# Weight conversion in turns of one operation: two in front of the transposes of a double step, one between transposes and scores

## Chip, core and metric

The kernel runs on one core of one Trainium2 chip. The metric is the device time of one execution in microseconds (us). The engines are named as in the profile: PE is TensorE (PEld its weight loads), DVE is VectorE, ACT is ScalarE, POOL is GpSimd, SP is SyncE, whose queue issues nearly all DMAs.

## What is computed

Attention over 4 batches and 8 heads with pooled queries, then a mixture of experts of which each token uses at most one, then a gated product of two linear layers and two more linear layers:

```python
q_pool = q.reshape(B, H, S // 2, 2, D).mean(axis=3)            # B=4, H=8, S=1152, D=64
scores = scale * np.matmul(q_pool, k.transpose(0, 1, 3, 2))
attn = softmax(scores)                                          # 576 x 1152 for each head
x = np.matmul(attn, v)                                          # -> 2304 tokens of 512
...                                                             # routing, experts
h = (x @ w1) * (x @ w2) @ w3                                    # inputs moe2_w1, moe2_w2, moe2_w3
out = h @ w_out                                                 # moe2_w_out
```

## The kernel before

The order of instructions on each engine is written by hand. The attention comes first, about the first half of the time. Its work is cut into 16 problems `p` (a batch and two heads) of 9 items each, so 144 items; an item is 128 rows of scores against all 1152 keys. The loop over `a` goes through the items two at a time. One pass is a **double step** and issues, in this order:

1. `emit_e` for items a-2 and a-1: ACT takes the exponential of an item's scores (L294), with the row maximum `sm` as its bias.
2. A first **turn** of the weight conversion, `side("DC")`, on DVE.
3. `emit_pv`: PE multiplies older, transposed items with V (L341). Up to 20 matmuls, by the table `PVU`; they wait for nothing that is new in this double step.
4. For items a-2 and a-1, `emit_t` and `emit_c`: PE transposes the exponentials into three PSUM banks (L305) and ACT, DVE, ACT copy one bank each into `pt` (L324). So DVE has one copy per item.
5. A second turn, again `side("DC")`.
6. For items a and a+1, `emit_s` and `emit_x`: PE computes scores into the same banks (L271), DVE reduces each item to its maximum (L282).

On DVE alone a double step therefore reads: two maxima, first turn, two copies, second turn, and the next two maxima. In the next double step the exponential waits for the first of these maxima, and the transposes for the exponential.

The weight conversion (`conv_ops`) has nothing to do with the attention. The last four weights come as 64-bit numbers and are turned into f32 in 40 pieces of 128 x 512, written to DRAM and read back after the attention. POOL squares the upper halves (L96, two pieces ahead); DVE then does four operations, L111, L112, L116 and L119, called **op 1 to op 4** below, each over 512 elements a lane. Op 4 releases the buffer `ch` for the load of a later piece (L91), and SP then stores the result. The generator yields at points in between, and `side` runs it up to the next yield: op 1 and op 2 stand in one piece, and op 3 and op 4 in one or in two, by turns (`if n % 2`). The routing of a batch (`route_ops`) shares these turns: in some double steps DVE does small routing operations in front of the conversion, and where routing is in its state `"D"` the conversion gets no turn.

POOL splits keys and queries of later problems at the same time (L224, L225, L230 to L238). All conversion is flushed before the last problem's items (`for _ in conv: pass`).

Of the kernel before, what the change touches and what calls it, by code (L numbers as in the profile page):

```python
# [17 lines left out]
NE, D, F = 8, 512, 1024  # L18
# [26 lines left out]
def body(ctx, tc, q, k, v, w9, w1, w2, m1, m2, w3t, wo, cst, mcst, ids, out, dbg=None):  # L45
# [29 lines left out]
    def c_src(name, c):  # L75
        if name == "w3t":
            return wsrc[name].rearrange("(a p f) t -> p a f t", p=128, f=F)[:, c % 8, CW * (c // 8):CW * (c // 8) + CW, :]
        return wsrc[name].rearrange("(p n) t -> p n t", p=128)[:, c * CW:(c + 1) * CW, :]

    def c_dst(name, c, t):  # L80
        if name == "w3t":
            u, a = 4 * (c // 8), c % 8
            SP.dma_start(wd[name].rearrange("(u p a f) -> p u a f", u=8, p=128, f=128)[:, u:u + 4, a],
                         t.rearrange("p (u f) -> p u f", u=4))
        else:
            SP.dma_start(wd[name].rearrange("(p n) -> p n", p=128)[:, c * CW:(c + 1) * CW], t)

    def conv_ops(erl):
        def ld(name, c):
            h = erl.tile([128, CW, 2], I32, tag="ch", name="ch", bufs=4)  # L90
            SP.dma_start(h, c_src(name, c))  # L91
            return h
        def sq(h):
            m = erl.tile([128, CW], F32, tag="cm", name="cm", bufs=3)
            hf = h.bitcast(F32)[:, :, 1]
            POOL.tensor_tensor(m, hf, hf, op=ALU.mult)  # L96
            return m

        nxt = [ld(*conv_q[i]) for i in range(3)]
        yield  # L100
        ms = [sq(nxt[0]), sq(nxt[1])]
        yield
        for n, (name, c) in enumerate(conv_q):
            h = nxt.pop(0)
            if n + 3 < len(conv_q):
                nxt.append(ld(*conv_q[n + 3]))
            a = erl.tile([128, CW], I32, tag="ca", name="ca", bufs=2)
            hf = h.bitcast(F32)[:, :, 1]
            m = ms.pop(0)
            u = m.bitcast(I32)  # L110
            DVE.scalar_tensor_tensor(m, m, TINY * TINY, hf, op0=ALU.is_ge, op1=ALU.mult)  # L111
            DVE.tensor_scalar(u, u, 0x07FFFFFF, 3, op0=ALU.bitwise_and, op1=ALU.logical_shift_left)  # L112
            yield
            if len(nxt) >= 2:
                ms.append(sq(nxt[1]))
            DVE.scalar_tensor_tensor(u, h[:, :, 1], -0x40000000, u, op0=ALU.bitwise_and, op1=ALU.bitwise_or)  # L116
            if n % 2:
                yield
            DVE.scalar_tensor_tensor(a, h[:, :, 0], 29, u, op0=ALU.logical_shift_right, op1=ALU.bitwise_or)  # L119
            c_dst(name, c, a.bitcast(F32))  # L120
            yield
# [13 lines left out]
    if True:  # L135
# [78 lines left out]
        def ld_kh(h):  # L214
            SP.dma_start(f(KH[0][64 * h:64 * h + 64]), f(KS[0][h][0:64]))
# [69 lines left out]
        def emit_e(i):  # L285
            p, l = divmod(i, NT9)
            b, hp = divmod(p, NHP)
            if (hp, l) == (0, 0):
                SM[b] = keep.tile([128, NHP, NT9], F32, tag="SM", name="SM", bufs=2)
            c = 8 if TILES[l] is None else 2 * TILES[l][1] + TILES[l][0]  # L290
            sp, sm = st_s.pop(i), st_m.pop(i)
            pt = mid.tile([128, 3, 384], F32, tag="p", name="p", bufs=3)
            st_p[i] = pt
            ACT.activation(pt, sp[:, :, 0:384], AF.Exp, bias=sm, scale=1.0, accum_out=SM[b][:, hp, c:c + 1])  # L294

        def emit_t(i, g, s, evac):
            p, l = divmod(i, NT9)
            hf = 0 if l < 5 else 1
            if g == 0 and l in (0, 5):
                PT[p, hf] = mid.tile([128, KT, 2, HN[hf]], F32, tag=f"pt{hf}", name=f"pt{hf}")  # L300
            src = st_p[i].rearrange("p a b -> p (a b)")
            tp = st_s[s][:, g]
            for u in range(3):
                kt = 3 * g + u
                m = PE.transpose(tp[:, u * 128:u * 128 + 128], src[:, kt * 128:kt * 128 + 128], ident)  # L305
                for e, _ in evac[:g]:
                    tc.declare_no_dep(m.ins, e, reason="other bank")
            st_t[i, g] = tp
            if g == 2:
                del st_p[i]  # L310
# [189 lines left out]
        conv = conv_ops(erl)  # L500
        rts = {}

        def side(kinds):
            k = rts.get("k")
            if k and k in kinds:
                rts["k"] = next(rts["g"], None)
            if kinds != "P" and k != "D":
                next(conv, None)

        def emit_meta(scratch):  # L510
# [240 lines left out]
        with tc.manual_schedule():  # L751
# [31 lines left out]
            def route_step(a, u):  # L783
                n = BANK[a % 18][u]
                if n is not None and rts.get("k") == "P":
                    free["b"] = VB[n]
                    side("P")

            for a in range(0, NSTEP + 8, 2):
                if a >= 44 and (a - 44) % 36 == 0 and (a - 44) // 36 < NB - 1:  # L790
                    rts["g"] = route_ops((a - 44) // 36)
                    rts["k"] = next(rts["g"])
                its = [i for i in (a - 2, a - 1) if 0 <= i < NSTEP]
                for i in its:
                    emit_e(i)
                route_step(a, 0)
                if a > 5:
                    side("DC")
                for pe in range(0, NP, 2):
                    for dp, hf, kt in PVU.get(a - 9 * pe, ()):  # L800
                        emit_pv(pe + dp, hf, kt)
                evac = {}
                for i in (a, a + 1):
                    if i < NSTEP or i - 2 in its:
                        st_s[i] = ps_s.tile([128, 3, 512], F32, tag="s", name="s")
                    evac[i] = []
                for i in its:
                    for g in range(3):
                        emit_t(i, g, i + 2, evac[i + 2])
                        emit_c(i, g, EV[g], evac[i + 2])  # L810
                if a > 5:
                    side("DC")
                route_step(a, 1)
                for i in (a, a + 1):
                    p, l = divmod(i, NT9)
                    ss = i < NSTEP
                    if i == NSTEP - NT9 + 1:
                        for _ in conv:
                            pass
                        ectx.close()  # L820
                        wfill = wprime_fill()
                    if i > NSTEP - NT9:
                        next(wfill, None)
                    if l == (4 if p == 0 else 1):
                        load(p + 2)
                    if l == 7 and p >= 1:
                        load_v(p + 1)
                    if ss:
                        for g in range(3):
                            emit_s(i, g, evac[i])  # L830
                        emit_x(i)
                        if i == 0:
                            prep_q(1, DVE, 0, 256, sq[1])
                            for c in range(3):
                                prep_k(1, 384 * c, 384 * c + 384)
                            ld_kh(1)
                            for h in range(2):
                                prep_q(h, POOL, 256, SQ, sr[h])
                            next(conv)
                            DVE.tensor_copy(base, cs[:, C_EOFF:C_EOFF + NC_])  # L840
                            DVE.tensor_copy(csr, cs[:, C_U:C_U + 256])
                        if i == 2:
                            PE.matmul(VB[1][:, 0:128], lhsT=ones, rhs=tri, start=True, stop=True)
                            DVE.tensor_copy(iota[:, 0:128], VB[1][:, 0:128])
                            DVE.tensor_scalar(iota[:, 128:NSL], iota[:, 0:NSL - 128], 128.0, None, op0=ALU.add)
                            DVE.tensor_scalar(idf, idt, 1.0, None, op0=ALU.add)
                    if ss and p == 0 and l < 3:
                        prep(1, l)
                    if i == 4:
                        next(conv)  # L850
                    if ss and l >= 6:
                        prep(p + 2, l - 6)
                    if ss and l in ((3, 4) if p == 0 else (4, 5)):
                        prep(p + 1, l if p == 0 else l - 1)
# [36 lines left out]
            n = 0  # L891
# [170 lines left out]
```

## Time and profile before

| What | us |
|---|---|
| median of 3 runs | 1062.84 (1062.28 to 1064.66) |
| the profiled execution, its own time | 1057.09 |
| its span in the profile | 1055.3 |
| granted PE clock, mean | 0.988 |
| attention, first to last row maximum | 10.4 to 516.6 |
| conversion on DVE, first op 1 to last op 4 | 33.1 to 462.3 |

A row of a timeline is one instruction, or several alike in succession: start, duration, engine, line, operation, output<-input, shapes, count, and in brackets the engine's idle time before it with what ended it. The chain of waits and the groups by line are read as sums over the whole span unless a stretch is named.

### The profile page before, as it was taken

The numbers are of one execution on the slowest core, as the hardware profiler recorded it, in microseconds if no ns is written. First come the engines' busy times: TensorE is split into PE (matmuls) and PEld (weight loads), VectorE is DVE, ScalarE is ACT, GpSimd is POOL, SyncE is SP. The second block draws the span as 40 slices with busy tenths as digits, with TensorE's granted clock in tenths as the row PEclk, the third lists the DMA queues.
The fourth block names the chain that finished last, engine by engine and source line by source line (L and its number), as shares of the span: only waits on it lengthen the run. The fifth ranks groups of instructions, "written<-read, shape, count | busy, mean of one in ns | idle before, by whom it ended". The sixth has DMA issues, their size and how long they took to land. (4 is left out here: it accounts for less than half of the span.)

```text
span 1055.3 us, 16801 instructions
## 1 busy us (share of the span) xinstructions
PE 1003.0 (95%) x6101; PEld 834.5 (79%) x6101; DVE 600.0 (57%) x934; ACT 460.7 (44%) x902; POOL 386.7 (37%) x426
## 2 busy tenths in 40 slices
PE   4899999999999999999999999996999999999996
PEld 3677777777777777787778788874989898989895
DVE  5888988789889898866554424256523131313120
ACT  3566566655665566666522324254422121212120
POOL 4752444582536743460801625167111101010101
PEclk8999999999999999999989999998999999999999
DMA  9887878579964687743416723233101010110000
GB/s 263 225 237 210 241 214 216 164 191 246 253 197 149 193 253 210 191 117 116 159 40 224 279 62 135 97 138 129 31 20 41 25 37 31 31 37 24 30 1 32
DMA packets 68237, 144.82 MB, mean 137 GB/s; under 512 B 12960, under 2 KB 22560, under 8 KB 68130
## 3 DMA queue, kind: packets, MB, share of 16 engines
q1 hardware_dynamic: 63330, 129.28, 42.5%
q0 software_dynamic: 4800, 14.24, 4.1%
q8 instruction: 52, 0.85, 0.3%
q14 instruction: 55, 0.45, 0.1%
HBM read 86.21 MB, written 22.87 MB: 103 GB/s over the span
## 5 line engine op out<-in xcount | busy, mean ns | idle before, releaser
L294 ACT ACTIVATE p<-s,sm 128x1152 f32<-128x1152 f32 x144 | 175.9, 1221 | 183.3 <-DVE sm L282 183.3
L282 DVE TENSOR_REDUCE sm<-s 128x1 f32<-128x1152 f32 x144 | 189.1, 1349 | 20.2 <-PE s L271 17.6
L305 PEld LDWEIGHTS s<-cs,p 128*128 128x128 f32 x1296 | 140.3, 142 | 65.3 <-ACT p L294 57.7
L305 PE MATMUL s<-cs,p 128*128 128x128 f32 x1296 | 167.9, 279 | 21.7 <-ACT p L294 19.2
L271 PE MATMUL s<-k,q 128*128 128x384 f32 x864 | 178.6, 348 | 7.9 <-DVE k L197 7.7
L271 PEld LDWEIGHTS s<-k,q 128*128 128x128 f32 x864 | 149.9, 191 | 10.2 <-DVE k L197 8.2
L341 PE MATMUL vb<-pt,vr 128*64 128x256 f32 (+1 forms) x1152 | 155.1, 412 | 0.0
L972 DVE TENSOR_TENSOR ar<-b,ar 128x384 f32<-128x384 f32 x48 | 26.7, 557 | 192.2 <-PE b L968 192.2
L324 ACT COPY pt<-s 128x384 f32<-128x384 f32 x288 | 122.5, 491 | 11.3 <-PE s L305 9.2
L341 PEld LDWEIGHTS vb<-pt,vr 128*64 128x64 f32 x1152 | 76.5, 136 | 59.3 <-issue 15.4
L987 POOL DMA_INDIRECT out_dram<-ar,slots x18 | 18.0, 1000 | 272.4 <-ACT ar L986 267.7
L324 DVE COPY pt<-s 128x384 f32<-128x384 f32 x144 | 79.2, 555 | 64.5 <-PE s L305 63.8
L225 POOL TENSOR_TENSOR kl<-kr,kh 128x384 fp32r<-128x384 f32 x45 | 47.8, 1062 | 77.7 <-DMA k<-kl 75.0
L973 ACT CAST CVh<-ar 128x384 fp32r<-128x384 f32 x48 | 24.6, 513 | 108.5 <-DVE ar L972 108.5
L96 POOL TENSOR_TENSOR cm<-ch 128x512 f32<-128x512 f32 x40 | 44.2, 1110 | 65.2 <-DVE ca L119 42.0
L563 PE MATMUL b<-W1h,CVh 128*128 128x512 f32 x176 | 60.1, 402 | 0.9 <-ACT CVh L694 0.7
L563 PE MATMUL b<-W2h,CVh 128*128 128x512 f32 x176 | 60.7, 405 | 0.1
L563 PE MATMUL b<-WPh,CVh 128*128 128x512 f32 x144 | 57.3, 398 | 0.0
L563 PE MATMUL b<-WPh,CVl 128*128 128x512 f32 x144 | 56.9, 395 | 0.0
L563 PE MATMUL b<-WPl,CVh 128*128 128x512 f32 x144 | 56.8, 395 | 0.0
L986 ACT COPY ar<-b 128x512 f32<-128x512 f32 x18 | 10.5, 586 | 86.2 <-PE b L563 86.2
L224 POOL TENSOR_SCALAR kh<-kr 128x384 fp32r<-128x384 f32 x45 | 27.3, 606 | 46.3 <-PE s L271 45.3
(210 smaller groups left out, 1810.8 us busy)
## 6 DMA issues: line engine op xcount, KB each, us to landing
R<-in_w_dram SPq DMA_DIRECT2D x16, 1024.0 KB, 7.5
vr<-in_v_dram SPq DMA_DIRECT2D x16, 576.0 KB, 6.3
kr<-in_k_dram SPq DMA_DIRECT2D x15, 576.0 KB, 6.7
qr<-in_q_dram SPq DMA_DIRECT2D x15, 576.0 KB, 6.6
k<-kh SPq DMA_DIRECT2D x30, 288.0 KB, 5.6
k<-kl SPq DMA_DIRECT2D x30, 288.0 KB, 7.0
q<-qnl SPq DMA_DIRECT2D x60, 144.0 KB, 5.1
ch<-in_w3t_dram SPq DMA_DIRECT2D x16, 512.0 KB, 6.7
```

What stands on the lines that cost most here:

```text
L96: POOL.tensor_tensor(m, hf, hf, op=ALU.mult)
L224: POOL.tensor_scalar(KH[i][:, cc], rawk[p][:, cc], 1.0, 0.0, op0=ALU.mult, op1=ALU.add)
L225: POOL.tensor_tensor(KL[:, cc], rawk[p][:, cc], f(KH[i][:, cc]), op=ALU.subtract)
L271: m = PE.matmul(sp[:, c, 0:384], lhsT=lt, rhs=kk[:, 384 * c:384 * c + 384], start=(n == 0), stop=(n == len(seq) - 1))
L282: DVE.tensor_reduce(sm, sp[:, :, 0:384], axis=AX.XY, op=ALU.max, negate=True)
L294: ACT.activation(pt, sp[:, :, 0:384], AF.Exp, bias=sm, scale=1.0, accum_out=SM[b][:, hp, c:c + 1])
L305: m = PE.transpose(tp[:, u * 128:u * 128 + 128], src[:, kt * 128:kt * 128 + 128], ident)
L324: m = (DVE.tensor_copy(o, i_) if eng is DVE else ACT.copy(o, i_)).ins
L341: PE.matmul(acc[64 * h:64 * h + 64, 0:n], lhsT=vr[:, h, kt, :], rhs=pt[:, kt, h, :], start=(kt == 0), stop=(kt == KT - 1))
L563: PE.matmul(o, lhsT=lh[a], rhs=rh[b_], start=(first and n == 0), stop=(last and n == len(order) - 1))
L972: DVE.tensor_tensor(cv, pb[:, 0:GT], av, op=ALU.mult)
L973: ACT.copy(CV[0][:, c], cv)
```

## The change

`conv_ops` now yields after each of its four operations, for every piece alike. `side` takes a number of operations: two in the first turn, one in the second, and one fewer of either where routing is in its state `"D"` (which before had no turn at all).

```diff
             DVE.scalar_tensor_tensor(m, m, TINY * TINY, hf, op0=ALU.is_ge, op1=ALU.mult)
+            yield
             DVE.tensor_scalar(u, u, 0x07FFFFFF, 3, op0=ALU.bitwise_and, op1=ALU.logical_shift_left)
             yield
             if len(nxt) >= 2:
                 ms.append(sq(nxt[1]))
             DVE.scalar_tensor_tensor(u, h[:, :, 1], -0x40000000, u, op0=ALU.bitwise_and, op1=ALU.bitwise_or)
-            if n % 2:
-                yield
+            yield
             DVE.scalar_tensor_tensor(a, h[:, :, 0], 29, u, op0=ALU.logical_shift_right, op1=ALU.bitwise_or)
...
-        def side(kinds):
+        def side(kinds, ops=0):
             k = rts.get("k")
             if k and k in kinds:
                 rts["k"] = next(rts["g"], None)
-            if kinds != "P" and k != "D":
+            if k == "D":
+                ops -= 1
+            for _ in range(ops):
                 next(conv, None)
...
                 if a > 5:
-                    side("DC")
+                    side("DC", 2)
...
                 if a > 5:
-                    side("DC")
+                    side("DC", 1)
```

The order of DVE's instructions shows what moves. The first place is two double steps early in the attention, those whose maxima start at 65.30 and 73.77 us in the trace; `sm<-s` are the maxima, `pt<-s` the copies of transposed exponentials, `cm` and `ca` the conversion. Before:

```order
L282 TENSOR_REDUCE sm<-s 128x1 x2
L111 SCALAR_TENSOR_TENSOR cm<-cm,ch 128x512
L112 TENSOR_SCALAR cm<-cm 128x512
L324 COPY pt_735<-s 128x3x128 x2
L116 SCALAR_TENSOR_TENSOR cm<-ch,cm 128x512
L119 SCALAR_TENSOR_TENSOR ca<-ch,cm 128x512
L282 TENSOR_REDUCE sm<-s 128x1 x2
L111 SCALAR_TENSOR_TENSOR cm<-cm,ch 128x512
L112 TENSOR_SCALAR cm<-cm 128x512
L324 COPY pt_735<-s 128x3x128 x2
L116 SCALAR_TENSOR_TENSOR cm<-ch,cm 128x512
L282 TENSOR_REDUCE sm<-s 128x1 x2
```

The same two double steps of the changed kernel (its L113, L117 and L119 are L112, L116 and L119 of before):

```order
L282 TENSOR_REDUCE sm<-s 128x1 x2
L119 SCALAR_TENSOR_TENSOR ca<-ch,cm 128x512
L111 SCALAR_TENSOR_TENSOR cm<-cm,ch 128x512
L324 COPY pt_734<-s 128x3x128 x2
L113 TENSOR_SCALAR cm<-cm 128x512
L282 TENSOR_REDUCE sm<-s 128x1 x2
L117 SCALAR_TENSOR_TENSOR cm<-ch,cm 128x512
L119 SCALAR_TENSOR_TENSOR ca<-ch,cm 128x512
L324 COPY pt_734<-s 128x3x128 x2
L111 SCALAR_TENSOR_TENSOR cm<-cm,ch 128x512
L282 TENSOR_REDUCE sm<-s 128x1 x2
```

In the first of these double steps op 3 and op 4 stood between the copies and the next maxima; now one operation stands there (op 2), and the first turn holds op 4 of one piece and op 1 of the next side by side. In the second, both kernels have two operations in the first turn and one in the second.

The second place is the end of the conversion, in the double steps at 453.05 and 459.82 us, where routing (`po`, `si`, `hl`, `pb`) has its own operations. Before:

```order
L428 TENSOR_TENSOR tp<-tp,cs 128x5
L429 TENSOR_TENSOR si<-tp,pb 128x5
L431 TENSOR_SCALAR hl<-si 128x10
L432 TENSOR_SCALAR hl<-si 128x10
L434 CAST hf<-hl 128x20
L282 TENSOR_REDUCE sm<-s 128x1 x2
L119 SCALAR_TENSOR_TENSOR ca<-ch,cm 128x512
L324 COPY pt_4972<-s 128x3x128 x2
```

And in the changed kernel:

```order
L282 TENSOR_REDUCE sm<-s 128x1 x2
L420 TENSOR_TENSOR pb<-pb,oh 128x5x8
L421 TENSOR_REDUCE po<-pb 128x5
L119 SCALAR_TENSOR_TENSOR ca<-ch,cm 128x512
L324 COPY pt_4817<-s 128x3x128 x2
```

The last op 4 stands one double step earlier, behind the routing's two operations of a turn in state `"D"`, which before held no conversion. PE's and ACT's instructions keep their order throughout.

## Rows read from the trace of the kernel before

**Rows 1.** The page: busy time and share of the span, instructions.

```profile
PE 1003.0 (95%) x6101; PEld 834.5 (79%) x6101; DVE 600.0 (57%) x934; ACT 460.7 (44%) x902; POOL 386.7 (37%) x426
```

**Rows 2.** Waits, whole span: who for whom, us in total, times, longest.

```profile
ACT p L294 <- DVE sm L282: 183.3, 79, 4.2
...
POOL cm L96 <- DVE ca L119: 42.0, 8, 7.4
```

**Rows 3.** Waits of PE from 30 to 466 us.

```profile
PE s L305 <- ACT p L294: 11.3, 20, 1.8
```

**Rows 4.** Waits of DVE from 30 to 466 us.

```profile
DVE pt L324 <- PE s L305: 46.3, 79, 1.4
DVE sm L282 <- PE s L271: 10.8, 26, 1.4
```

**Rows 5.** Timeline of DVE, two double steps without stretched operations.

```profile
134.82 2.62 DVE L282 TENSOR_REDUCE sm<-s 128x1 f32<-128x1152 f32 x2 [0.17 <-PE s L271]
...
140.36 0.68 DVE L116 SCALAR_TENSOR_TENSOR cm<-ch,cm 128x512 int32<-128x512 int32 x1
141.07 0.69 DVE L119 SCALAR_TENSOR_TENSOR ca<-ch,cm 128x512 int32<-128x512 int32 x1
141.68 2.61 DVE L282 TENSOR_REDUCE sm<-s 128x1 f32<-128x1152 f32 x2
144.21 0.68 DVE L111 SCALAR_TENSOR_TENSOR cm<-cm,ch 128x512 f32<-128x512 f32 x1
144.93 0.43 DVE L112 TENSOR_SCALAR cm<-cm 128x512 int32<-128x512 int32 x1
145.34 0.56 DVE L324 COPY pt<-s 128x384 f32<-128x384 f32 x1
146.61 0.56 DVE L324 COPY pt<-s 128x384 f32<-128x384 f32 x1 [0.71 <-PE s L305]
147.08 0.68 DVE L116 SCALAR_TENSOR_TENSOR cm<-ch,cm 128x512 int32<-128x512 int32 x1
148.06 1.36 DVE L282 TENSOR_REDUCE sm<-s 128x1 f32<-128x1152 f32 x1 [0.30 <-PE s L271]
```

**Rows 6.** Timeline of all engines, the double steps from 65.30 and 73.77 us.

```profile
65.30 2.62 DVE L282 TENSOR_REDUCE sm<-s 128x1 f32<-128x1152 f32 x2 [0.28 <-PE s L271]
...
70.73 1.28 DVE L116 SCALAR_TENSOR_TENSOR cm<-ch,cm 128x512 int32<-128x512 int32 x1
...
71.42 1.87 POOL L230 TENSOR_TENSOR qsum<-qr 128x576 f32<-128x576 f32 x1
...
72.05 1.80 DVE L119 SCALAR_TENSOR_TENSOR ca<-ch,cm 128x512 int32<-128x512 int32 x1
...
73.77 2.61 DVE L282 TENSOR_REDUCE sm<-s 128x1 f32<-128x1152 f32 x2
...
76.51 2.47 PE L305 MATMUL s<-cs,p 128*128 128x128 f32 x18 [1.57 <-ACT p L294]
...
77.77 0.97 PEld L305 LDWEIGHTS s<-cs,p 128*128 128x128 f32 x9 [0.30 <-ACT p L294]
```

**Rows 7.** Timeline of PE: the first and last of nine late groups of transposes.

```profile
41.09 2.46 PE L305 MATMUL s<-cs,p 128*128 128x128 f32 x18 [0.37 <-ACT p L294]
...
365.75 2.47 PE L305 MATMUL s<-cs,p 128*128 128x128 f32 x18 [0.34 <-ACT p L294]
```

**Rows 8.** Op 1 (L111): shortest, median, longest ns of one, first and last start.

```profile
L111 DVE SCALAR_TENSOR_TENSOR cm<-cm,ch x40: 673/684/1884, 33.1 to 431.6; 128x512 f32<-128x512 f32 x40
```

**Rows 9.** Timeline of DVE, a first turn that was stretched.

```profile
111.30 1.87 DVE L111 SCALAR_TENSOR_TENSOR cm<-cm,ch 128x512 f32<-128x512 f32 x1
...
113.55 1.01 DVE L324 COPY pt<-s 128x384 f32<-128x384 f32 x2
114.48 0.93 DVE L116 SCALAR_TENSOR_TENSOR cm<-ch,cm 128x512 int32<-128x512 int32 x1
115.33 1.34 DVE L282 TENSOR_REDUCE sm<-s 128x1 f32<-128x1152 f32 x1
```

## The prediction

> **What bounds the kernel now.** I read the page first: PE is busy 95% of the span and DVE 57% [rows 1], which alone would leave little for a change on DVE. Then the chain of waits, where one entry is large: ACT's exponential waited 183.3 us for DVE's row maximum [rows 2]. The question is whether that wait reaches PE. It does, but rarely: in the stretch with conversion (30 to 466 us, 62 double steps) PE itself stood idle 11.3 us in 20 places before the transposes, waiting for the exponential [rows 3]. So DVE has its say only where it is late with a maximum.
>
> When it is late is seen in the timeline of DVE. A double step, counted from its first maximum to the next one's, takes 148.06 - 141.68 = 6.38 us where the second turn has one operation; DVE then waits 0.30 us for PE's scores, so DVE isn't last [rows 5]. The double step ahead of it has two operations in the second turn, takes 141.68 - 134.82 = 6.86 us, and its closing maximum starts with no idle mark: DVE was last [rows 5]. Over the stretch DVE shows such a wait before its maxima only 26 times in 62 double steps [rows 4]; in the others the second turn ended last, or about together with the scores. The copies between the turns are different: DVE waited for their transposes 79 times, 46.3 us in all, 0.59 us each [rows 4]. The first turn therefore has slack, the second has not.
>
> It is worst where an operation is stretched. Op 1 takes 684 ns at the median and up to 1884 [rows 8]. In the double step from 65.30 us op 3 takes 1.28 and op 4 1.80 us, while POOL runs a 1.87 us addition; the double step lasts 8.47 us, and in the next PE stands idle 1.57 us before its transposes and its weight loads 0.30 us more between the two items [rows 6].
>
> **The change, part by part.** The order of before and after gives the counts, over all 160 operations. Second turns: 83 operations before, 52 after. First turns: 77 before, 108 after. Before, 31 double steps had two operations in the second turn; after, none has. The work on DVE stays the same, and the last op 4 comes one double step earlier, because the turns in routing's state "D" now take one. SP's stores and loads of the conversion go with op 4 and op 1, in the same order; the flush before the last problem finds nothing in either kernel.
>
> *Term 1, nine double steps where PE stands idle because DVE was late.* I compared each maximum's start with the end of the score matmuls of its item and took the lateness that one operation less removes, but at most what PE lost. The nine idle marks (the first and last in [rows 7], the largest in [rows 6]) add up to 6.55 us, and the wait of 0.30 us between the two items [rows 6] mostly goes as well: up to 9 x 0.30 = 2.7 us. Bounds: 9.25 us if all goes, about 4.5 if the one operation left is itself stretched by a microsecond every time. I take 9.0, since in all nine the removed operation, or the exchange of a stretched op 3 or 4 for the short op 2, is about as long as the loss.
>
> *Term 2, seven double steps like that at 134.82*, with two hardly stretched operations: between 0.28 and 0.53 us each; the pair in [rows 5] shows 0.48. Taken at 0.39: 2.7 us.
>
> *Term 3, ten double steps* in which DVE was last by 0.05 to 0.15 us (op 1 and op 2 in the second turn, 0.68 + 0.43 us, just do not fit): 0.9 us.
>
> *Term 4, a longer first turn.* Two operations take 0.68 + 0.43 or at most 0.69 + 0.68 us, and behind the former the first copy starts at once while the second still waits 0.71 us [rows 5]: the 31 added operations are hidden by that wait and cost nothing when not stretched. If that cover went, each would cost up to its 0.7 us. A stretched first turn exists already: op 1 at 1.87 us, after which the copies run without a wait and the closing maximum starts with no idle mark [rows 9], some 0.1 us late. I charge 1.0 us for a few more of these.
>
> *Term 5, op 4 and op 1 side by side.* POOL's square waits for op 4 through its buffer in 8 of 40 pieces [rows 2] and then runs beside the next operation on DVE. Before, a copy or a maximum always stood between op 4 and op 1. After, 11 first turns have op 1 directly behind op 4. At that rate two of 11 would meet a square, at 1.88 - 0.68 = 1.2 us each if op 1 is stretched fully, nothing if not; partly hidden, as in term 4. Charged: 1.5 us.
>
> Sum: 9.0 + 2.7 + 0.9 - 1.0 - 1.5 = 10.1 us. The profiled execution took 1057.09 us and would take 1047.0. The median of the runs shown lies 5.75 us above it; the same 10.1 us off 1062.84 gives **1052.7**. Of what follows the attention nothing moves.
>
> Behind term 5 stands a rule of the Trainium skill that speaks against the change: "GPSIMD Engine Reference", section "Key points", says that GpSimd shares its SBUF interfaces with VectorE and contends with VectorE instructions that have two SBUF inputs or run in a 2-port mode. The stretched op 3 and op 4 beside POOL's addition agree with it [rows 6]. Taken as a rule for every conversion operation, it would let the longer first turns pay wherever POOL works, which is the first rival below; by the rows here many such meetings cost nothing, and the sum goes by those.
>
> **The rivals.**
> *A: the stretches move along.* The first turn becomes the place where DVE meets POOL. For it: op 1 reaches 1.88 us [rows 8], and DVE is full in those double steps, so a late first turn makes copies, scores and maximum late. Against: the stretched turn of [rows 9] cost next to nothing. Price: all 11 adjacent pairs stretched by 1.2 us, 0.7 of it hidden by the copies' wait [rows 5], 5.5 us; and 2 to 3 us in other first turns. The gain falls to about 4 us: 1058.8.
> *B: PE is the bound after all.* PE's busy share is 95% [rows 1], and matmuls with V wait for nothing, so what DVE gives back would turn into PE's waiting elsewhere. For it: 62 double steps contain only 11.3 us of idle PE [rows 3], of which the longest, 1.8 us, is at the start, with no V work yet. Against: the 1.57 us [rows 6] sit right behind a late maximum. Time: about 1062, no change.
> *C: slower, by late copies.* If the two operations of a first turn took more than about 2.1 us as a rule (1.37 plus the 0.71 us of cover [rows 5]), the second copy would end late in every double step and PE would stop between the scores' banks. With 27 stretched turns at 0.6 us past that point, 16 us come in and 12.6 go out: 1066. Against: 1.37 us is what the parts add up to.
> *D: the change doesn't do what it says*, its three operations a double step leaving conversion for the flush. The order excludes it: all 40 op 4 stand well ahead.
>
> **How the numbers follow.** My forecast 0.70, its own times 1048 to 1057; A 0.15; B 0.09; C 0.05; D 0.01. What a measurement of this kernel can tell from no change is about 0.2%, 2.1 us. Faster: the forecast and A, and a little of B, 0.86. Same: most of B, a tail of A, 0.08. Slower: C and D, 0.06. The range runs from all three gains whole, no new cost and the 0.30 us between the items gone in ten more double steps (12.6 + 3.0 us, 1047.2) to A with its costs a quarter larger (12.6 - 10.6 us, about 1061); B, C and D outside it hold 0.15.
>
> **What would show it.** In the profile after: PE's wait before the transposes, 11.3 us in 20 places, falls to about 5 in 12 or fewer, mostly those with few V matmuls; DVE waits for scores before the maxima in far more than 26 double steps; ACT's 183.3 us falls by 10 or more; the last maximum starts about 10 us earlier than 516.6. DVE's wait for transposes before its copies falls well below 46.3 us, as the first turn now fills it. Op 1's mean rises if term 5 holds. Wrong I would be if the copies began to run without a wait in most double steps and PE's score matmuls showed waits for DVE's copies (then C or A), or if PE's idle vanished and the double steps stayed as long (then B).

## The result

The changed kernel took 1053.32 us (median; 1050.70 to 1055.22 over 5 runs) beside 1062.28 us (1060.34 to 1064.66) for the kernel before: ratio 0.9914, 95% interval 0.9889 to 0.9939. A second comparison of the same two kernels gave 0.9932 (0.9907 to 0.9956). The forecast was 1052.7 us, with a range of 1047 to 1061.

Of the profile after, first the page: busy time and share of the span, beside [rows 1]. The span is 1048.9 us.

```profile
PE 1003.8 (96%) x6101; PEld 836.7 (80%) x6101; DVE 598.5 (57%) x934; ACT 462.7 (44%) x902; POOL 388.5 (37%) x426
```

All engines do the same work in the same busy time, within 2 us each; what changed is who waits. Waits of the whole span (who for whom, us, times, longest), beside [rows 2]:

```profile
ACT p L294 <- DVE sm L282: 169.6, 80, 3.4
...
POOL cm L96 <- DVE ca L119: 50.8, 12, 8.5
```

Waits of PE over the stretch with conversion (30 to 456 us here), beside [rows 3]:

```profile
PE s L305 <- ACT p L294: 4.5, 9, 1.8
PE s L271 <- DVE pt L324: 0.3, 1, 0.3
```

and of DVE, beside [rows 4]:

```profile
DVE pt L324 <- PE s L305: 28.1, 54, 1.0
DVE sm L282 <- PE s L271: 21.1, 44, 1.4
```

The reader sees the exchange. PE's wait in front of the transposes fell from 11.3 us in 20 places to 4.5 in 9. DVE now waits for scores in front of its maxima 44 times in place of 26, so it is last less often; and it waits less for transposes in front of its copies, 28.1 us in place of 46.3, as the first turn fills that wait.

The double steps from 65.30 and 73.77 us of [rows 6] are those from 63.86 and 70.26 us here. A timeline of all engines:

```profile
63.86 2.62 DVE L282 TENSOR_REDUCE sm<-s 128x1 f32<-128x1152 f32 x2 [0.28 <-PE s L271]
...
66.40 0.68 DVE L119 SCALAR_TENSOR_TENSOR ca<-ch,cm 128x512 int32<-128x512 int32 x1
...
67.00 1.50 DVE L111 SCALAR_TENSOR_TENSOR cm<-cm,ch 128x512 f32<-128x512 f32 x1
...
68.42 1.01 DVE L324 COPY pt<-s 128x384 f32<-128x384 f32 x2
...
69.35 0.90 DVE L113 TENSOR_SCALAR cm<-cm 128x512 int32<-128x512 int32 x1
...
70.26 2.62 DVE L282 TENSOR_REDUCE sm<-s 128x1 f32<-128x1152 f32 x2
...
72.38 0.67 POOL L234 TENSOR_SCALAR qnh<-qsum 128x576 fp32r<-128x576 f32 x1
...
72.80 0.78 DVE L117 SCALAR_TENSOR_TENSOR cm<-ch,cm 128x512 int32<-128x512 int32 x1
...
73.13 1.73 POOL L235 TENSOR_TENSOR qnl<-qsum,qnh 128x576 fp32r<-128x576 f32 x1
73.43 2.18 PE L305 MATMUL s<-cs,p 128*128 128x128 f32 x18
...
73.62 1.79 DVE L119 SCALAR_TENSOR_TENSOR ca<-ch,cm 128x512 int32<-128x512 int32 x1
...
75.33 1.01 DVE L324 COPY pt<-s 128x384 f32<-128x384 f32 x2
...
76.26 1.22 DVE L111 SCALAR_TENSOR_TENSOR cm<-cm,ch 128x512 f32<-128x512 f32 x1
...
77.40 2.61 DVE L282 TENSOR_REDUCE sm<-s 128x1 f32<-128x1152 f32 x2
```

The first double step takes 6.40 us in place of 8.47: its second turn is one operation of 0.90 us, where two of 1.28 and 1.80 stood. PE's transposes at 73.43 no longer show an idle mark (1.57 us before). The second double step now has the stretched op 4, 1.79 us, in its first turn, and takes 7.14 us. Before it took 80.14 - 73.77 = 6.37 us, as its successor's maxima show:

```profile
80.14 2.62 DVE L282 TENSOR_REDUCE sm<-s 128x1 f32<-128x1152 f32 x2 [0.30 <-PE s L271]
```

The pair together is down from 14.84 to 13.54 us.

The last row maximum starts here (shortest, median, longest ns; first and last start):

```profile
L282 DVE TENSOR_REDUCE sm<-s x144: 1335/1349/1359, 10.5 to 506.9; 128x1 f32<-128x1152 f32 x144
```

516.6 - 506.9 = 9.7 us were gained in the attention. PE's granted clock isn't behind it: in the attention it was lower only in the kernel before, 0.50 from 16.2 to 23.0 us, and the maxima of the first double step with conversion start at 30.56 us there and at 30.86 here. The span gained only 1055.3 - 1048.9 = 6.4 us: 3.3 us were lost behind it, where no instruction differs. In windows at equal distance from the last maximum (30 to 60, 60 to 90 and 215 to 235 us behind it), the column ahead of the DMA share is PE's granted clock. Before:

```profile
546.60:576.60 30.00, 28.86 (x125) 23.61 (x126) 15.94 (x52) 4.05 (x6) 0.99 (x1) 0.89 0.47 146
576.60:606.60 30.00, 27.45 (x135) 21.85 (x134) 15.66 (x19) 13.03 (x25) 19.57 (x19) 1.00 0.82 295
731.60:751.60 20.00, 15.51 (x79) 15.54 (x80) 13.26 (x16) 8.39 (x14) 5.31 (x4) 0.83 0.17 45
```

and after:

```profile
536.90:566.90 30.00, 28.88 (x132) 23.57 (x133) 16.03 (x53) 5.47 (x9) 0.54 (x1) 0.94 0.49 155
566.90:596.90 30.00, 26.86 (x123) 20.92 (x122) 15.19 (x19) 11.13 (x21) 19.61 (x19) 0.94 0.78 280
721.90:741.90 20.00, 13.74 (x62) 13.34 (x63) 12.87 (x16) 9.84 (x15) 5.69 (x5) 0.74 0.19 46
```

PE was granted the lower of its two levels, 1.2 GHz, for part of these windows, around gaps in its work (13.74 us busy of 20 in the last), and for a different part each time. The missing clock times the length adds up to 6.7 us before and 8.8 after, a difference of 2.1 us. But other profiles of this study don't bear the clock out as the cause. In the last run with second turns in some double steps the same windows have 0.89, 1.00 and 0.83, as in the kernel before, and the stretch from the last maximum to the end of the span takes 541.0 us, not 538.7; with the spare operation in the first turn they have 0.94, 0.94 and 0.76, and it takes 539.0. Over all 14 profiles it was 538.7 to 542.2 us, and not in step with the attention's length. What varies there stays open. So below the last maximum's start stands beside the ratios: it leaves this out.

### The profile page after: what moved, and what is told of

Same layout as the page of the kernel before. It is cut to its first block, busy times and chain, and to the rows that moved or that the text cites. A ratio compares the mean times of both kernels' runs of the same rounds, so it can differ in the third digit from the quotient of the medians.

```text
span 1048.9 us, 16795 instructions
## 1 busy us (share of the span) xinstructions
PE 1003.8 (96%) x6101; PEld 836.7 (80%) x6101; DVE 598.5 (57%) x934; ACT 462.7 (44%) x902; POOL 388.5 (37%) x426
## 5 line engine op out<-in xcount | busy, mean ns | idle before, releaser
L324 ACT COPY pt<-s 128x384 f32<-128x384 f32 x288 | 124.0, 490 | 13.4 <-PE s L305 10.1
L988 ACT COPY ar<-b 128x512 f32<-128x512 f32 x18 | 10.6, 586 | 86.2 <-PE b L565 86.2
```

The lines of the kernel that those rows point to most:

```text
L324: m = (DVE.tensor_copy(o, i_) if eng is DVE else ACT.copy(o, i_)).ins
```

## Experiments

The theory: a conversion operation costs by its place. In front of the maxima it makes them late, and through the exponential PE; in front of the copies it lies in a wait. The rivals: the gain is that of smaller pieces meeting GpSimd's work less; or the turns in state "D"; or late copies eat it. Each ratio is to the kernel before; the changed kernel's last maximum is at 506.9 us, and at 509.2 in a second profile (506 to 508 were expected of it). So differences of some 2 us between two profiles mean nothing here.

**Turns exchanged.**

```diff
-                    side("DC", 2)
+                    side("DC", 1)
...
-                    side("DC", 1)
+                    side("DC", 2)
```

> The changed kernel with the turns exchanged: one operation in the first turn, two in the second. If the place of the operation decides (the second turn stands in front of the maxima, the first behind a wait of the copies), nearly every double step with conversion is late as the two-operation ones of before were: 0.1 us where op 1 and op 2 meet there, 0.3 to 0.5 us for the other pairs, more where stretched; the last maximum starts at 517 to 527 us and the time is 1062 to 1072 us, no better than before. If the finer cut itself gives the gain (single operations that meet GpSimd's work less), the time stays within 3 us of the changed kernel's 1053.

Measured: 1.0070 (1.0044 to 1.0096), 1068.42 us, last maximum at 527.4 us. The same pieces at the other place are 18 to 20 us worse in the attention than in the two profiles of the changed kernel, and slower than the kernel before. Waits of DVE from 30 to 470 us:

```profile
DVE pt L324 <- PE s L305: 67.9, 110, 2.3
DVE sm L282 <- PE s L271: 3.7, 8, 2.2
```

DVE waits for scores in front of its maxima 8 times: it is nearly always last there. The finer cut gives nothing by itself.

**All three in the first turn.**

```diff
-                    side("DC", 2)
+                    side("DC", 3)
...
-                    side("DC", 1)
+                    side("DC", 0)
```

> All three operations in the first turn, none in the second. By the place theory the lateness that is left in the changed kernel (about 3 us of waits before and between the transposes) goes, and the first turn of 2.05 us just fits its cover of about 2.1 us where nothing is stretched; where it is, copies and scores come late. Sum: 1050 to 1056 us, score matmuls waiting for copies in some ten double steps. If the first turn has no cover beyond two operations (the late-copies rival), every double step loses 0.3 us or more: 1060 to 1075 us.

Measured: 1.0001 (0.9982 to 1.0020), last maximum at 517.5 us: the gain is gone, outside both expected ranges. Waits of PE from 30 to 470 us:

```profile
PE s L271 <- DVE pt L324: 7.7, 10, 1.9
PE s L305 <- ACT p L294: 4.6, 9, 1.8
```

DVE now waits for scores in front of its maxima 63 times, so the maxima are seldom late, but a new wait has come, of the scores for DVE's copies. PE's wait for the exponential was expected to go and hasn't: 4.6 us in 9 places, as in the changed kernel. The longest new wait, on DVE:

```profile
129.07 1.50 DVE L117 SCALAR_TENSOR_TENSOR cm<-ch,cm 128x512 int32<-128x512 int32 x1
130.61 1.79 DVE L119 SCALAR_TENSOR_TENSOR ca<-ch,cm 128x512 int32<-128x512 int32 x1
132.32 1.15 DVE L111 SCALAR_TENSOR_TENSOR cm<-cm,ch 128x512 f32<-128x512 f32 x1
133.39 1.01 DVE L324 COPY pt<-s 128x384 f32<-128x384 f32 x2
```

and on PE:

```profile
131.51 0.60 PE L271 MATMUL s<-k,q 128*128 128x384 f32 x2
133.99 3.34 PE L271 MATMUL s<-k,q 128*128 128x384 f32 x10 [1.88 <-DVE pt L324]
```

Three stretched operations take 4.4 us, the copies begin only when the transposes are long done, and the scores stop after two matmuls. PE's granted clock behind this stop was 0.54 (134.0 to 137.4 us), so the ten matmuls left took 3.34 us (at 124.77 us twelve took 2.33). All ten waits stand in double steps in which at least one operation of the first turn took more than 1 us. So the late-copies mechanism is real: one wait of 0.3 us with two operations, ten with three.

**One more operation, in either turn.** A spare operation of the kind of op 1, 512 elements, in 62 double steps; the edit of the first, and of the second in its place:

```diff
+        def extra(a):
+            if 5 < a < 130:
+                DVE.scalar_tensor_tensor(spare, spare, 1.0, spare, op0=ALU.mult, op1=ALU.max)
...
                     side("DC", 2)
+                    extra(a)
```

> The changed kernel with one more VectorE operation of the same kind (512 elements, two inputs in SBUF, on a spare tile) at the end of the first turn of 62 double steps, 62 x 0.68 = 42 us of VectorE work. By the place theory the copies' wait for transposes (28 us left in 54 places) covers most of it: 2 to 8 us slower than the changed kernel, 1055 to 1061 us. If VectorE's total work decides, 15 us or more: above 1068 us.

> The same added operation, at the end of the second turn instead. By the place theory it stands in front of the maxima with 0.1 to 0.3 us of cover, so 0.35 to 0.55 us for each of 62 double steps: 20 to 35 us slower than the changed kernel, 1073 to 1088 us. If VectorE's total work decides and not the place, the same time as with the operation in the first turn, within 3 us.

Measured: 1.0046 (1.0026 to 1.0065) in the first turn, 1.0147 (1.0108 to 1.0186) in the second; last maximum at 522.5 and 531.1 us. Against the changed kernel's 506.9 that is 15.6 us, 0.25 us an operation, and 24.2 us, 0.39 us (13.3 and 21.9 us against its second profile). The second is as expected. The first is not: it is dearer than the 2 to 8 us of the place theory, and in the attention about the 15 us that were expected if DVE's total work decided, though the time is below the 1068 us of that case. What speaks for the place is that the same work costs 8.6 us more in the second turn. The first turn's price comes with late copies, as in the run above. PE's waits with the operation in the first turn:

```profile
PE s L271 <- DVE pt L324: 7.7, 13, 1.4
PE s L305 <- ACT p L294: 7.5, 15, 1.8
```

and in the second:

```profile
PE s L305 <- ACT p L294: 19.5, 34, 1.8
...
PE s L271 <- DVE pt L324: 0.2, 1, 0.2
```

Each place has its own wait: behind the second turn the wait for the exponential grows, from 4.8 us in 10 places in the changed kernel over the same stretch, behind the first mainly that for the copies, from 0.3 us.

**No turn in state "D".**

```diff
-                ops -= 1
+                ops = 0
```

> The changed kernel without a conversion turn in routing's state D, as before: the conversion lasts until the flush with 52 or so operations in second turns all the same. If the turns in state D carry part of the gain, it loses 2 us or more of it; by the place theory they are free room and nothing else, and the time stays within 2 us of the changed kernel's.

Measured: 0.9896 (0.9860 to 0.9931), last maximum at 507.6 us, between the changed kernel's two. The median of its 4 runs is 1048.57 us beside 1052.96 of the changed kernel's 6, further below than the 2 us expected, but the intervals overlap: it is no slower, and whether it is faster stays open. The turns in state "D" aren't where the gain is.

**Second turns only in some double steps.** Twice, with two operations in every first turn and the conversion spread to the flush; first where V's matmuls are widest, then in the others (`not in`):

```diff
-            if k == "D":
-                ops -= 1
+            if k == "D" and ops == 1:
+                ops = 0
...
-                    side("DC", 1)
+                    side("DC", int(a % 18 in (6, 8, 14, 16)))
```

> The changed kernel with an operation in the second turn only in the 4 of 9 double steps after whose maxima the matmuls with V are widest (so that PE has work while DVE is late); first turns keep two operations, in routing's state D too, and the conversion lasts until the flush. 29 operations in second turns in place of 52. By the place theory what is left of PE's waits before and between the transposes falls by 2 to 4 us and nothing else changes: the last maximum at 503 to 506 us, 1 to 4 us faster than the changed kernel. If the waits that are left in the changed kernel come from long first turns (stretched by GpSimd), it is no faster, or slower by what the longer conversion meets.

> The mirror image of the run with second turns where V's matmuls are widest: an operation in the second turn only in the other 5 of 9 double steps, those in which GpSimd splits no keys or queries and the added operation took 0.70 us in place of 1.05. First turns of two operations throughout, state D included; the conversion lasts until the flush. If what is left of DVE's lateness in the changed kernel comes from second turns stretched beside GpSimd, PE's waits before and between the transposes fall by 2 to 4 us: the last maximum at 503 to 506 us, 0.987 to 0.991 of the kernel before. If it comes from stretched first turns or is no lateness at all, the same as the changed kernel: the last maximum at 507 to 510 us, 0.991 to 0.994.

Measured: 0.9928 (0.9900 to 0.9955) with the last maximum at 509.7 us, and 0.9934 (0.9913 to 0.9956) at 508.3. Neither beats the changed kernel, run beside the first of them at 0.9932, so the 503 to 506 us of the place theory were missed in both. In the second, DVE waits for scores 57 times in place of 46 over the same stretch, but PE's wait in front of the transposes is still 4.9 us in 12 places (4.8 in 10): what is left of that wait doesn't come from the second turns taken away.

**The added second-turn operation, by double step.** The spare operation only where V's matmuls are widest (28 double steps), or only in the others (34):

```diff
-            if 5 < a < 130:
+            if 5 < a < 130 and a % 18 in (6, 8, 14, 16):
```

> The changed kernel with the added operation at the end of the second turn in those 28 double steps only after whose maxima the matmuls with V are widest (a mod 18 in 6, 8, 14, 16). If a late maximum costs only what PE's matmuls with V don't cover, most of the 0.68 us is hidden there: 0.1 to 0.25 us each, 3 to 7 us slower than the changed kernel. If every late maximum costs its lateness, 0.4 us each as the 62 together showed: 11 us slower.

> The same in the other 34 double steps only. If PE's cover decides, nearly all of the lateness shows: 0.45 to 0.6 us each, 15 to 20 us slower than the changed kernel. If every late maximum costs alike, 0.4 us each: 14 us slower, close to 34/28 of the run with the wide ones.

Measured: 1.0049 (1.0028 to 1.0070), last maximum at 521.4 us; and 1.0038 (1.0019 to 1.0056), 518.1 us. That is 14.5 us or 0.52 an operation where PE's cover is best, and 11.2 us or 0.33 where it is worst: the opposite of what was expected (0.44 and 0.26 against the second profile). In time the two runs are alike. The spare operation itself points to the reason. By line (count, busy, mean ns), where V's matmuls are widest:

```profile
L507 DVE SCALAR_TENSOR_TENSOR spare<-spare 128x512 f32<-128x512 f32 x28 | 29.5, 1054 | 0.0
```

and in the others:

```profile
L507 DVE SCALAR_TENSOR_TENSOR spare<-spare 128x512 f32<-128x512 f32 x34 | 23.8, 699 | 0.0
```

Two of the four kinds of double step with the widest matmuls (`a % 18` of 8 and 16) are those in which GpSimd splits keys and queries for 6 to 7 us; there the spare operation took 1.20 and 1.45 us on average, and in the other two kinds 0.77 and 0.80.

**Short operations.** Op 1 to op 3 over 8 elements in place of 512, in the changed kernel and in the one before; op 4, squares, loads and stores stay.

```diff
-            DVE.scalar_tensor_tensor(m, m, TINY * TINY, hf, op0=ALU.is_ge, op1=ALU.mult)
+            DVE.scalar_tensor_tensor(m[:, 0:8], m[:, 0:8], TINY * TINY, hf[:, 0:8], op0=ALU.is_ge, op1=ALU.mult)
```

> The changed kernel with op 1 to op 3 over 8 elements in place of 512 (the converted weights are not converted then, so the output after the expert layers is not the reference's); op 4, squares, loads and stores stay. What the conversion still costs the attention: by the place theory the last maximum comes at 499 to 503 us, 4 to 8 us ahead of the changed kernel's 506.9; if the conversion were hidden by now, within 2 us of it.

> The kernel before with op 1 to op 3 over 8 elements in place of 512 (its weights aren't converted then, so its output after the expert layers isn't the reference's), to see whether both kernels have the same floor. By the place theory the turns no longer matter, and the last maximum comes within 2 us of the 504 us that the changed kernel had with the same operations shortened. If the changed order gains by something else than the length of the second turn, such as what GpSimd or the DMA queue do when, it stays 5 us or more above that.

One execution each: last maximum at 504.0 and 506.7 us, spans 1045.3 and 1048.4. The first is 2.9 us ahead of the changed kernel (5.2 of its second profile), between the two cases of its expectation. It isn't the attention without conversion: an operation over 8 elements still takes 0.25 to 0.32 us on average, op 4 is whole, and DVE spends 65.6 us on the conversion in place of 124.0. PE's wait from 30 to 470 us is then

```profile
PE s L305 <- ACT p L294: 3.9, 8, 1.8
```

beside 4.8 us in 10 places in the changed kernel, so nearly all of what was left of this wait has another cause than the length of these operations. Seven of its nine places in the changed kernel's stretch are in the kernel before too, with the same length to 0.02 us: one at the start, the others every nine double steps. The two orders differ by 2.7 us with short operations, again between the two cases: most of the 9.7 us goes with the length of the turns. From one execution each, and with 2.3 us between two profiles of one kernel, the 2.7 us can be chance; whether op 4 has a part in them was not tried.

## Why the prediction held

**The bottleneck.** DVE's lateness at the maxima was what reached PE: exchanging the turns alone made the kernel slower than before, and each spare operation in front of the maxima cost 0.39 us. Rival B, that PE is the bound anyway, falls with PE's wait from 11.3 to 4.5 us and the attention shorter by 9.7.

**Term 1, 9.0 us.** Of the nine marked places one still has a mark in the profile after, of 0.34 us. The PE timeline shows it, and one mark that is at none of the nine:

```profile
265.64 2.47 PE L305 MATMUL s<-cs,p 128*128 128x128 f32 x18 [0.34 <-ACT p L294]
...
390.75 2.47 PE L305 MATMUL s<-cs,p 128*128 128x128 f32 x18 [0.51 <-ACT p L294]
```

So 6.55 - 0.34 = 6.2 us of idle went, and in seven of the nine the wait of 0.30 us between the items too, 2.1 us: 8.3 of the 9.0.

**Terms 2 to 5** were to give 2.7 + 0.9 - 1.0 - 1.5 = 1.1 us, and 9.7 - 8.3 = 1.4 is left for them, which measures none of them. A second count goes by the length of each double step, from its first maximum to the next one's. In the stretch with conversion the nine are 9.3 us shorter together, the other 23 with two operations in the second turn before are 2.5 us shorter (terms 2 and 3: 3.6), and the remaining 30 are 2.0 us longer (terms 4 and 5: 2.5). In the second profile it is 7.8, 1.6 and 1.7. So the groups came out near their forecast, though a late maximum shifts time between neighbours, and the single steps did not. The example of term 2, a double step of 6.86 us before, takes 6.84 after (from 130.57 us), as the end of it on DVE shows:

```profile
136.26 1.22 DVE L119 SCALAR_TENSOR_TENSOR ca<-ch,cm 128x512 int32<-128x512 int32 x1
137.41 2.61 DVE L282 TENSOR_REDUCE sm<-s 128x1 f32<-128x1152 f32 x2
```

One operation stands in the second turn, but stretched to 1.22 us; the maxima still start without an idle mark. Scores wait for copies 0.3 us in one place, 1.3 us in three in the second profile (term 4: 1.0). Term 5 had the count about right and the cause wrong: in 11 places op 1 stands directly behind an op 4, and in three of them (four in the second profile) it was stretched, by 0.5 to 0.8 us, but behind GpSimd's splitting of keys and queries (the one at 67.00 us above ends 0.55 us behind such an instruction), none behind the square that op 4 releases. The square waits for op 4 in 12 pieces in place of 8, yet op 1's mean fell from 913 to 839 ns (888 in the second profile), where I had it rise; op 3's rose, from 777 to 857 (830).

**Luck.** The second profile had the last maximum at 509.2 us, a gain of 7.4 us in place of 9.7, and the second comparison gained 0.7%, some 7.2 us: the agreement of the median to 0.6 us is closer than the terms deserve. "Nothing moves" behind the attention was not so in the profile, by 3.3 us.

**Rivals A and C** did not decide, with two operations in the first turn. Three bring late copies: the last maximum is 10.6 us later than in the changed kernel (8.3 than in its second profile). The cover of 2.1 us was added up wrongly: the 0.71 us of [rows 5] were left behind a first turn of 0.68 + 0.43 us, not behind 1.37, so the cover there is about 1.8 us. In the run with three operations 0.42 + 0.69 + 0.69 = 1.80 us, from 109.14 us, left the second copy a wait of 0.19 us, so 2.0. Either holds two operations of at most 1.37 us, so term 4's argument stands for quiet double steps; three, of up to 2.05 us, are at its edge even there, and well over it where GpSimd stretches them, where all ten waits were.

**The rule on the shared interfaces** (the Trainium skill, "GPSIMD Engine Reference", section "Key points") proved the better guide for the size of a slot's price: the spare operation, with two SBUF inputs, at 1.054 against 0.699 us agrees with it. It did not turn the sum, as the changed kernel has no more operations, and they were stretched about as much: the means of op 1 to op 4 add up to 3.10 us in place of 3.12 (3.14 in the second profile).

## What to carry to other kernels

In a loop of several engines, filler work on one of them is priced by the slot it stands in: look for the wait that the engine has anyway, count its length in double steps where other engines share its memory as well as in quiet ones, and fill it to that length and not beyond. Two operations in the slot that had a wait and one in the slot that had none gained 0.7 to 0.9%; three and none gained nothing, one and two lost 0.7%. When a gain in one stage doesn't arrive whole at the end, compare the later stages at equal distance from an event that both traces share, before looking for a cause in the change, and do it over several profiles: the clock fitted one pair here and failed the next.

## What the runs showed of the hardware

Conversion operations on DVE and GpSimd's instructions excluded each other as wholes. In the timeline of the changed kernel, POOL's L234 ends at 72.38 + 0.67 = 73.05 us and DVE's op 3 at 73.58; POOL's L235 ends at 74.86 and DVE's op 4 at 75.41: each 0.53 to 0.55 us behind POOL's end, however early the DVE operation had begun. This holds throughout the trace: of the 160 conversion operations 49 took more than 0.76 us (op 2: 0.50), and 48 of these end a nearly fixed time behind the end of a POOL instruction, 0.53 to 0.55 us for the operations with two inputs in SBUF and 0.28 to 0.29 for op 2, which has one. An example of op 2, where POOL ends at 262.69 us and DVE at 262.97:

```profile
261.27 1.42 POOL L235 TENSOR_TENSOR qnl<-qsum,qnh 128x576 fp32r<-128x576 f32 x1
261.50 1.47 DVE L113 TENSOR_SCALAR cm<-cm 128x512 int32<-128x512 int32 x1
```

It goes both ways: L235 took 1.73 us from 73.13 us, and 1.41 at 193.72 us, beside a maximum. The maxima, read from PSUM, took 1.335 to 1.359 us in all 144 cases, beside POOL or not. The Trainium skill, "Perfetto Trace Analysis", section "Optimizing Scalar/DVE Operations", says that the two share an SBUF read port, which a 2-port VectorE operation holds as an exclusive lock; the rows agree, and show it for operations with two tensor inputs too.
